# k and v in two runs of five tokens per partition pair, and k^T v from 20 matmuls of 128 rows

## The chip, the cores and the metric

One core of a Trainium2 chip runs the whole program. The metric is the device time of one execution in microseconds; the kernel before has a median of 1215.24 us over three runs (1215.23 to 1216.68).

## What is computed

Linear attention without a softmax feeds two feed-forward blocks. The change touches the attention alone: for each of 4 x 8 heads, 576 tokens of width 64.

```python
def _attn_ref(q, k, v, g_norm):          # (4, 8, 576, 64) each
    kv = np.einsum('bhsd,bhse->bhde', k, v)
    out = np.einsum('bhsd,bhde->bhse', q, kv)
    rms = np.sqrt(np.mean(out * out, axis=-1, keepdims=True) + 1e-06)
    return (out / rms * g_norm).astype(np.float32)

def reference(...):
    x = attention, as (2304, 512)
    x = _moe_ref(x)      # x @ w_in, h * clip(h + 3, 0, 6) / 6, @ w_out; 512 -> 2048 -> 512
    return _moe2_ref(x)  # 4 experts, 512 -> 1024 -> 512, weighted by domain_probs
```

## The kernel before

The attention runs in eight stages (NHB = 2 B), each of four heads of one batch. Loads, products and the rest are issued in an order written out by hand (`manual_schedule`) on PE, ACT, DVE and SP; GpSimd is left out of that order.

`att_load(i)` brings q, k and v of stage i, each with one load of 576 KB. Head pair r lies in the free dimension; the head's parity x and a group of nine tokens (CJ = 9) make the partition: partitions 0 to 63 hold the even head, 64 to 127 the odd one, and each has nine consecutive tokens of 64 values (2304 bytes). Six buffers are used in turn, so stage i + 2 reuses those of stage i. `paced` makes a load wait, from the twelfth on, for an earlier load to have landed, so that some three are under way; the weights of the first feed-forward block (`load_raw`) are in the same order of loads.

`att_q(i)` transposes q on PE. `att_kv(i)` forms k^T v: for each of nine tokens j, two parities x and two pairs r one matmul of 64 rows by 64 columns, 36 in all, accumulated in PSUM (`kvp`); the half of the partitions that a result lands on is half[x ^ r], so that the four quarters of the array are used in turn. In float32 each matmul is two passes in the trace, 72 in all. ACT copies the result to `kvd`, `att_out(i)` multiplies q by it, `att_rms(i)` normalises on ACT and DVE, and `att_x(i - 1)` transposes the stage before into the feed-forward block's operands (xH, xL).

Stage i of the loop does, in this order on PE: att_out(i), att_q(i + 1), att_kv(i + 1), then a part of a feed-forward tile (`ff_mm`, `ff_in`) or filler matmuls (`warm`), and att_x(i - 1). On SP stand att_load(i + 2) and some weight loads. `convert(n)` turns raw weights into operands, on ACT and DVE, with two of its steps on GpSimd for the first three halves (POOLED, lines 171 and 174). After the eighth stage the rest of the feed-forward blocks follows.

Of the kernel before, what the change touches and what calls it, by code (L numbers as in the profile page):

```python
# [8 lines left out]
F32 = mybir.dt.float32  # L9
# [3 lines left out]
ALU = mybir.AluOpType  # L13
AX = mybir.AxisListType
# [3 lines left out]
def kernel(  # L18
# [18 lines left out]
    nc = tc.nc  # L37
    B, H, S, D = q.shape
    NT, DM = out.shape
    E = moe2_w1.shape[0]  # L40
    P = 128
# [5 lines left out]
    CP = P // 2  # L47
    CJ = S // CP
    CB = TB // CP
    HH = H // 2  # L50
    NP = HH // 2
# [10 lines left out]
    LAG = 3  # L62
    RATE = (4200, 3000, 2600, 2900, 0)
    FMAX = 3.0e38
    PADL, PADR = 232, 248

    const = ctx.enter_context(tc.tile_pool(name="const", bufs=1))
    sp = ctx.enter_context(tc.tile_pool(name="sp", bufs=1))
# [28 lines left out]
    ident = const.tile([P, P], F32, name="ident")  # L97
    three = const.tile([P, 1], F32, name="three")
    eps4 = const.tile([P, 1], F32, name="eps4")
    gcol = const.tile([P, 1], F32, name="gcol")  # L100
    dp = const.tile([P, B, CJ, E], F32, name="dp")
    psum_e = const.tile([P, B, CJ], F32, name="psum_e")
    prob = const.tile([P, NTT, E], F32, name="prob")
# [12 lines left out]
    FREE, NEAR = 11, 13  # L116
    flow = []

    def paced(dma):
        flow.append(dma.ins)  # L120
        if len(flow) > FREE and not done[0]:
            tc.add_manual_dep(
                dma.ins, flow[-3 if len(flow) <= NEAR else -4].name,
                mybir.DependencyInfo(mybir.DependencyClass.Sync, mybir.DependencyReason.DATA), reason="paced")

    todo = [(n, h) for n in range(len(ftiles)) for h in range(2)]

    def load_raw():
        if not todo:
            return  # L130
        n, h = todo.pop(0)
        u, f = ftiles[n]
        g = sum(UNITS1[:u]) + f
        r = rawp.tile([P, KD * P, 2], U32, tag="raw", name="raw")
        if h == 0:
            paced(nc.sync.dma_start(
                out=r.rearrange("p (c f) w -> p c (f w)", c=KD),
                in_=moe_w_in.bitcast(U32)[:, 2 * g * P:2 * (g + 1) * P].rearrange("(c p) f -> p c f", p=P)))
        else:
            paced(nc.sync.dma_start(  # L140
                out=r.rearrange("p e w -> p (e w)"), in_=moe_w_out.bitcast(U32)[g * P:(g + 1) * P, :]))
        raw[n, h] = r
# [40 lines left out]
    st = {}  # L183
    natile = [0]

    def att_load(i):
        b, hf = divmod(i, 2)
        t = {}
        for nm, src in (("q", q), ("k", k), ("v", v)):
            m = natile[0] % 6  # L190
            natile[0] += 1
            pool, tag = (accp, "acc") if m < 5 else (wp, f"w{m - 1}")
            t[nm] = pool.tile([P, NP, CJ, D], F32, tag=tag, name=f"{nm}in")
            paced(nc.sync.dma_start(
                out=t[nm].rearrange("p r j d -> p r (j d)"),
                in_=src[b, hf * HH:(hf + 1) * HH].rearrange("(r x) (s j) d -> (x s) r (j d)", x=2, j=CJ),
            ))
        st[i] = t


    half = [slice(x * D, (x + 1) * D) for x in range(2)]
# [33 lines left out]
    def att_kv(i):  # L235


        t = st[i]
        kvp = t["kvp"]
        for j in range(CJ):  # L240
            for x in range(2):
                for r in range(NP):
                    nc.tensor.matmul(  # L243
                        kvp[half[x ^ r], r, :D], lhsT=t["k"][half[x], r, j, :], rhs=t["v"][half[x], r, j, :],
                        start=(j == 0), stop=(j == CJ - 1))
        nc.scalar.activation(out=kvd[i % 2][:, 0], in_=kvp[:, :, :D], func=AF.Copy)
        for y in range(2):
            nc.scalar.activation(out=kvd[i % 2][half[y], 1], in_=kvp[half[1 - y], :, :D], func=AF.Copy)
# [183 lines left out]
    start = {}  # L432
    last = {}
# [5 lines left out]
    done = [False]  # L439
# [32 lines left out]
    def warm(starts):  # L472
        z = psa.tile([P, DM], F32, tag="a0", name="zp")
        for o in starts:
            nc.tensor.matmul(z, lhsT=zero[:, o:o + P], rhs=zero, start=True, stop=True)

    warm((0,) * 8)

    att_load(0)
    load_raw()  # L480
    make_identity(nc, ident)
    nc.gpsimd.memset(three, 3.0)
    nc.gpsimd.memset(eps4, 0.25e-6)

    nc.scalar.activation(out=gcol, in_=three, func=AF.Sqrt)
    att_load(1)
    load_raw()
    nc.sync.dma_start(out=gcol[0:D, :], in_=g_norm.rearrange("(p o) -> p o", o=1))
# [5 lines left out]
    with tc.manual_schedule(engines=engines):  # L494
        qc = att_q(0)
        for x in qc[:2]:
            x()
        warm((0,) * 4)
        att_kv(0)
        qc[2]()  # L500
        warm((0,) * 2)
        conv(6)
        for i in range(NHB):
            if i + 2 < NHB:
                att_load(i + 2)
# [4 lines left out]
            if i == NHB - 2:  # L510
                for y in range(2):
                    nc.sync.dma_start(
                        out=dp[half[y]],
                        in_=moe2_domain_probs.rearrange("(b s j) e -> s b j e", b=B, j=CJ))
# [9 lines left out]
            if nxt:  # L524
                att_kv(i + 1)
                qc[2]()
            fin = [nop] * 4
            kvp = st[min(i + 1, NHB - 1)]["kvp"]
# [66 lines left out]
        for y in range(2):  # L595
            h = half[y]
            for jp in range(2):
                j = slice(2 * y + jp, CJ - 1, 4)
                nc.vector.tensor_tensor(
                    out=prob[h, :B * HH].rearrange("p (b a) e -> p b a e", b=B)[:, :, 2 * jp:2 * jp + 2],  # L600
                    in0=dp[h, :, j], in1=psum_e[h, :, j].unsqueeze(3).to_broadcast([D, B, 2, E]), op=ALU.mult)
            nc.vector.tensor_tensor(
                out=prob[h, B * HH:], in0=dp[h, y::2, CJ - 1],
# [239 lines left out]
    first = build(0)  # L843
# [70 lines left out]
```

## Time and profile before

| | us |
|---|---|
| median of three runs | 1215.24 |
| the profiled execution's own time | 1216.68 |
| span of the profiled execution | 1214.9 |
| eight k^T v products (line 243), first and last start | 8.2 and 62.8 |

The span is what the profiler's records cover; the time of an execution has 1.8 us around it. The profile shows one execution. Its parts are the busy time of each engine, the same by stretches, the chain of work that ended last followed back from the end, what each engine waited for, and the transfers with their packets. PE's weight loads (PEld) run beside its matmuls (PE). "issue" stands for time in which an engine waited for nothing that the profile shows.

### The profile page before, as it was taken

The page shows a single profiled execution, that of the slowest core. Times are in us where ns is not written, and L with a number is a line of the kernel's source. Part 1 is how long each engine was busy: PE and PEld are TensorE (multiplying, and loading weights), DVE is VectorE, ACT ScalarE, POOL GpSimd, SP SyncE. Part 2 cuts the span into 40 slices and gives each one's busy share as a digit, 9 for nine tenths or more (in the row PEclk, how much of TensorE's full clock was granted, in tenths as well). Part 3 has the DMA queues.
Part 4 walks back from the last instruction along what each step waited for, and adds up shares of the span by engine and source line. Part 5 has one row for each costly group of instructions (what it writes and reads, how often), then busy time and mean ns, then how long its engine had stood idle before and what let it go on. Part 6 is the DMA issues. An engine that isn't in the chain of part 4 may idle for free.

```text
span 1214.9 us, 17426 instructions
## 1 busy us (share of the span) xinstructions
PE 1193.9 (98%) x6999; PEld 1053.5 (87%) x6999; DVE 770.4 (63%) x1455; ACT 581.9 (48%) x1116; POOL 8.9 (1%) x16
## 2 busy tenths in 40 slices
PE   7899999999999999999999999999999999999997
PEld 6778888888888899999999889999999899999996
DVE  5889999953533755565656585656565856565652
ACT  5776555622422434444444554444445644444441
POOL 2000000000000000000000000000000000000000
PEclk9999999999999999999999999999999999999999
DMA  8812222300200012222111132222222422221202
GB/s 287 290 36 70 87 87 74 100 1 1 70 1 1 1 35 71 70 70 70 70 69 62 61 105 69 70 70 70 70 70 70 122 70 70 70 70 70 70 1 52
DMA packets 59345, 87.18 MB, mean 72 GB/s; under 512 B 3712, under 2 KB 36480, under 8 KB 59264
## 3 DMA queue, kind: packets, MB, share of 16 engines
q1 hardware_dynamic: 59264, 86.07, 21.6%
q8 instruction: 55, 0.90, 0.3%
q14 instruction: 26, 0.21, 0.1%
HBM read 81.34 MB, written 4.72 MB: 71 GB/s over the span
## 4 chain that ended last, share of the span: by engine, by line
PE 93%; DVE 3%; DMA 2%; ACT 1%; issue 1%; SPq 0%; DVEq 0%
PE po L748 32%; PE po L388 15%; PE qa L781 14%; PE qb L781 14%; PE ph L353 5%; PE ph L355 5%; PE ph L354 5%; DMA vin<-in_v_dram 2%; DMA qin<-in_q_dram 1%; DVE xl L311 1%; DVE acc L764 1%; PE kvp L243 0%; DVE r L367 0%; DVE ssq L274 0%; ACT xh L310 0%
## 5 line engine op out<-in xcount | busy, mean ns | idle before, releaser
L748 PE MATMUL po<-wout,g 128*128 128x512 f32 x1728 | 402.1, 390 | 0.0
L748 PEld LDWEIGHTS po<-wout,g 128*128 128x128 f32 x1728 | 323.6, 188 | 65.4
L781 PE MATMUL qb<-xs,win 128*128 128x384 f32 x1008 | 203.4, 336 | 1.2 <-ACT us L822 1.2
L781 PE MATMUL qa<-xs,win 128*128 128x384 f32 x1008 | 203.1, 336 | 0.0
L388 PE MATMUL po<-gH,w 128*128 128x512 f32 (+1 forms) x632 | 191.3, 368 | 0.2 <-ACT gH L369 0.2
L781 PEld LDWEIGHTS qb<-xs,win 128*128 128x128 f32 x1008 | 178.1, 188 | 4.0 <-ACT us L822 1.8
L781 PEld LDWEIGHTS qa<-xs,win 128*128 128x128 f32 x1008 | 178.3, 188 | 2.2 <-ACT us L822 0.2
L655 DVE TENSOR_TENSOR wout<-raw,wout 128x512 fp32r<-128x512 f32 x96 | 62.2, 688 | 171.2 <-ACT wout L654 171.2
L654 ACT ACTIVATE wout<-raw 128x512 fp32r<-128x512 f32 x96 | 55.4, 624 | 226.7 <-PE po L748 226.7
L388 PEld LDWEIGHTS po<-gH,w 128*128 128x128 f32 x632 | 115.7, 188 | 20.5 <-ACT gH L369 0.6
L353 PE MATMUL ph<-xh,w 128*128 128x512 f32 (+1 forms) x320 | 118.4, 370 | 0.0
L354 PE MATMUL ph<-xl,w 128*128 128x512 f32 (+1 forms) x320 | 117.9, 368 | 0.0
L355 PE MATMUL ph<-xh,w 128*128 128x512 f32 (+1 forms) x320 | 117.8, 368 | 0.0
L388 PE MATMUL po<-gL,w 128*128 128x512 f32 (+1 forms) x316 | 116.3, 368 | 0.0
L366 ACT ACTIVATE r<-ph,three 128x512 f32<-128x512 f32 (+1 forms) x80 | 51.5, 643 | 135.0 <-PE ph L355 134.8
L367 DVE SCALAR_TENSOR_TENSOR r<-r,ph 128x512 f32<-128x512 f32 (+1 forms) x80 | 50.6, 632 | 89.3 <-ACT r L366 88.8
L811 DVE SCALAR_TENSOR_TENSOR g<-sums,g 128x384 fp32r<-128x384 f32 x96 | 53.6, 558 | 81.4 <-ACT g L808 81.4
L808 ACT ACTIVATE g<-cs 128x384 fp32r<-128x384 f32 x96 | 50.4, 525 | 63.5 <-DVE cs L824 54.4
L654 ACT ACTIVATE win<-sums 128x512 fp32r<-128x512 f32 x96 | 60.7, 633 | 40.2 <-DVE sums L667 37.8
L811 DVE SCALAR_TENSOR_TENSOR g<-cs,g 128x384 fp32r<-128x384 f32 x96 | 53.4, 556 | 27.3 <-ACT g L808 27.3
L353 PEld LDWEIGHTS ph<-xh,w 128*128 128x128 f32 x320 | 60.3, 188 | 10.4
L369 ACT ACTIVATE gH<-r 128x512 fp32r<-128x512 f32 (+1 forms) x80 | 47.1, 589 | 46.1 <-DVE r L367 46.1
(129 smaller groups left out, 1275.4 us busy)
## 6 DMA issues: line engine op xcount, KB each, us to landing
raw<-in_moe_w_dram SPq DMA_DIRECT2D x96, 512.0 KB, 4.1
raw<-in_moe_w_in_dram SPq DMA_DIRECT2D x16, 512.0 KB, 3.7
raw<-in_moe_w_out_dram SPq DMA_DIRECT2D x16, 512.0 KB, 3.5
qin<-in_q_dram SPq DMA_DIRECT2D x8, 576.0 KB, 5.3
kin<-in_k_dram SPq DMA_DIRECT2D x8, 576.0 KB, 6.2
vin<-in_v_dram SPq DMA_DIRECT2D x8, 576.0 KB, 6.3
out_dram<-acc SPq DMA_DIRECT2D x36, 128.0 KB, 2.3
dp<-in_moe_domain_probs_dram SPq DMA_DIRECT2D x2, 36.0 KB, 4.2
```

What stands on the lines that cost most here:

```text
L353: nc.tensor.matmul(ph, lhsT=w[:, 0, c, :], rhs=xH[t][:, c, :], start=(c == 0), stop=False)
L354: nc.tensor.matmul(ph, lhsT=w[:, 0, c, :], rhs=xL[t][:, c, :], start=False, stop=False)
L355: nc.tensor.matmul(ph, lhsT=w[:, 1, c, :], rhs=xH[t][:, c, :], start=False, stop=(c == KD - 1))
L366: lambda: nc.scalar.activation(out=r, in_=ph, func=AF.Relu, bias=three[:, 0:1]),
L367: lambda: nc.vector.scalar_tensor_tensor(out=r, in0=r, scalar=6.0, in1=ph, op0=ALU.min, op1=ALU.mult),
L388: nc.tensor.matmul(po_t[u, t][o], lhsT=lhsT, rhs=rhs, start=(f == 0 and m == 0), stop=(f == UF[u] - 1 and m == 2))
L654: nc.scalar.activation(out=dst[0], in_=src, func=AF.Copy)
L655: nc.vector.tensor_tensor(out=dst[1], in0=src, in1=dst[0].bitcast(F32), op=ALU.subtract)
L748: nc.tensor.matmul(ps[i], lhsT=lhsT, rhs=w[:, f, y], start=(j == 0 and f == 0 and m == 0), stop=(j == FP - 1 and f == 1 and m == 2))
L781: nc.tensor.matmul(bank, lhsT=w[:, wy, AOP[m], c], rhs=xs[m][:, xy, c], start=first and n == 0, stop=n == 5, skip_group_check=True)
L808: nc.scalar.activation(out=g[f][:, 0, t], in_=src, func=func)
L811: nc.vector.scalar_tensor_tensor(out=g[f][:, 1, t], in0=src, scalar=0.0, in1=g[f][:, 0, t].bitcast(F32), op0=ALU.max, op1=ALU.subtract)
```

## The change

k and v of a stage are held in [128, 4 heads, 5 tokens, 64]: two neighbouring partitions share nine tokens, the even one holds tokens 0 to 4 and the odd one 4 to 8. Each head has a load of its own, 128 rows of 1280 bytes, so k and v take four loads of 160 KB each. The fifth token of the nine is there twice; GpSimd multiplies slot 0 of k by a column `even` that is 1 on even partitions and 0 on odd ones, in place. The product is 5 slots x 2 pairs x 2 heads = 20 matmuls that use all 128 rows and 64 columns; slot 0 comes last. `paced` counts four loads as one group. The identity is made ahead of the first loads, since `even` is summed from it on DVE. q is loaded as before.

```diff
-    PADL, PADR = 232, 248
+    PADL, PADR = 224, 248
...
+    even = const.tile([P, 1], F32, name="even")
...
-    def paced(dma):
-        flow.append(dma.ins)
-        if len(flow) > FREE and not done[0]:
+    def paced(dma, first=True, last=True):
+        if first and len(flow) >= FREE and not done[0]:
             tc.add_manual_dep(
-                dma.ins, flow[-3 if len(flow) <= NEAR else -4].name,
+                dma.ins, flow[-2 if len(flow) < NEAR else -3].name,
                 mybir.DependencyInfo(mybir.DependencyClass.Sync, mybir.DependencyReason.DATA), reason="paced")
+        if last:
+            flow.append(dma.ins)
...
+    JG, JP = CJ // 2 + 1, CJ // 2
...
+            if nm != "q":
+                t[nm] = pool.tile([P, HH, JG, D], F32, tag=tag, name=f"{nm}in")
+                for h in range(HH):
+                    first = src[b, hf * HH + h, 0, 0:1]
+                    dma = nc.sync.dma_start(
+                        out=t[nm][:, h].rearrange("p j d -> p (j d)"),
+                        in_=bass.AP(first.tensor, first.offset, [[CJ * D, CP], [JP * D, 2], [1, JG * D]]))
+                    paced(dma, h == 0, h == HH - 1)
+                continue
...
-        for j in range(CJ):
-            for x in range(2):
-                for r in range(NP):
+        nc.gpsimd.tensor_scalar(
+            out=t["k"][:, :, 0, :], in0=t["k"][:, :, 0, :], scalar1=even[:, 0:1], scalar2=None, op0=ALU.mult)
+        for j in (*range(1, JG), 0):
+            for r in range(NP):
+                for x in range(2):
                     nc.tensor.matmul(
-                        kvp[half[x ^ r], r, :D], lhsT=t["k"][half[x], r, j, :], rhs=t["v"][half[x], r, j, :],
-                        start=(j == 0), stop=(j == CJ - 1))
+                        kvp[half[x ^ r], r, :D], lhsT=t["k"][:, 2 * r + x, j, :], rhs=t["v"][:, 2 * r + x, j, :],
+                        start=(j == 1), stop=(j == 0))
...
+    make_identity(nc, ident)
+    nc.vector.tensor_reduce(
+        out=even, in_=ident.rearrange("p (s y) -> p y s", y=2)[:, 0, :], axis=AX.X, op=ALU.add)
     att_load(0)
     load_raw()
-    make_identity(nc, ident)
```

## Rows read from the trace of the kernel before

**Rows 1.** The page, part 1: busy us of each engine, share, instructions.

```profile
PE 1193.9 (98%) x6999; PEld 1053.5 (87%) x6999; DVE 770.4 (63%) x1455; ACT 581.9 (48%) x1116; POOL 8.9 (1%) x16
```

**Rows 2.** Stretches: us, length, busy us (instructions) per engine, granted clock, DMA share, GB/s.

```profile
20.00:25.00 5.00, 3.12 (x87) 2.58 (x85) 4.40 (x11) 2.98 (x9) 2.55 (x2) 1.00 0.63 202
...
50.00:55.00 5.00, 5.00 (x164) 4.41 (x163) 4.84 (x9) 3.30 (x7) 1.01 (x1) 1.00 0.94 333
...
100.00:110.00 10.00, 10.00 (x45) 8.27 (x45) 9.97 (x19) 5.58 (x9) 0.00 (x0) 1.00 0.34 101
```

**Rows 3.** The chain that ended last, in order of time: start us, us, what.

```profile
22.33 7.89 DMA vin<-in_v_dram
...
30.36 1.28 PE kvp L243 x72
...
34.58 1.42 issue
...
38.45 1.01 PE kvp L243 x57
39.46 1.67 issue
41.13 0.46 PE kvp L243 x15
...
62.15 0.43 issue
```

**Rows 4.** Waits of PE in the first 70 us: in total us, times, longest.

```profile
PE kvp L243 <- DMA vin<-in_v_dram: 3.6, 3, 1.7
```

**Rows 5.** PE's instructions up to the two holes (stretches), and PE's instruction queue, 0 to 70.

```profile
28.10:34.70 6.60, 6.04 (x126) 5.05 (x127) 4.22 (x10) 4.68 (x11) 0.00 (x0) 1.00 0.79 237
35.90:39.70 3.80, 3.46 (x127) 3.11 (x127) 2.80 (x7) 2.71 (x6) 0.00 (x0) 1.00 0.89 291
...
q8 instruction: 10, 0.16, 1.1%
```

**Rows 6.** The product's line: one stage as a stretch; all passes, ns min/median/max; waits.

```profile
30.30:31.70 1.40, 1.28 (x72) 1.17 (x72) 1.00 0.88 300
...
L243 PE MATMUL kvp<-vin,kin x576: 213/218/268, 8.2 to 62.8; 64*64 64x64 f32 x192
...
L243 PEldq EVENT_SEMAPHORE  x8: 51/51/51, 7.7 to 60.2; - x8
```

**Rows 7.** Eight passes on 128 rows and columns: timeline, and their weight loads.

```profile
69.20 1.05 PE L564 MATMUL kvp<-ident 128*128 128x128 f32 x8
...
L564 PEld LDWEIGHTS kvp<-ident x8: 187/192/192, 69.0 to 69.9; 128*128 128x128 f32 x8
```

**Rows 8.** Packets, 2.5 to 7 us, and of one lone load, 92 to 97: count, MB, share.

```profile
DMA packets 792, 1.69 MB, mean 375 GB/s; under 512 B 41, under 2 KB 73, under 8 KB 792
...
q1 hardware_dynamic: 792, 1.69, 98.4%
...
q1 hardware_dynamic: 528, 0.52, 34.0%
```

**Rows 9.** SP's timeline, two issues; the second one's us from issue to landing.

```profile
1.23 0.46 SPq L194 DMA_DIRECT2D kin<-in_k_dram  x1
...
31.52 0.37 SPq L194 DMA_DIRECT2D vin<-in_v_dram  x1
...
vin<-in_v_dram SPq DMA_DIRECT2D x1, 576.0 KB, 6.7
```

**Rows 10.** GpSimd's timeline: start us, us, what.

```profile
1.35 0.10 POOL L482 MEMSET three<- 128x1 f32 x1
...
1.51 0.29 POOL masks.py:199 TENSOR_SCALAR_AFFINE_SELECT ident<-ident 128x128 f32<-128x128 f32 x1
...
53.99 1.27 POOL L171 TENSOR_TENSOR r<-r,x 128x512 f32<-128x512 f32 x1 [30.61 <-ACT qT L228]
```

**Rows 11.** Waits of SP's queue in the first 90 us: in total us, times, longest.

```profile
SPq L194 <- DMA kin<-in_k_dram: 18.5, 5, 9.4
...
SPq L489 <- DMA kin<-in_k_dram: 0.4, 1, 0.4
```

## The prediction

> **What bounds the kernel now.** I read the page's first part first: PE is busy 98% of the span, DVE 63%, ACT 48% [rows 1]. Whatever an edit saves on PE's path is therefore worth its full length, and so is whatever it adds. Then the busy time by stretches: from 100 us on PE has no idle time (10.00 of 10), while in the attention stretch it has gaps (3.12 of 5 between 20 and 25 us, with the DMA engines at 0.63) [rows 2]. The edit lies wholly in that stretch, the first 63 us, so the question is by how much the eighth k^T v product ends earlier or later; all behind it is unchanged and moves with it.
>
> The chain of work in order of time tells what limits that stretch [rows 3]. Up to 30.2 us it is loads: the fourth v, issued at 22.33, took 7.89 us to land, and the product of that stage began at 30.36. PE waited for v three times, 3.6 us in all [rows 4]. After that the chain is compute: PE, ACT, DVE in turn, and between 50 and 55 us DVE is busy 4.84 of 5 [rows 2]. In between stand three holes named "issue", where PE waited for nothing that the profile shows: 1.42, 1.67 and 0.43 us [rows 3]. The middle one cuts a product in two, after 57 of its 72 passes. PE has 126 matmuls and 127 weight loads in the stretch that ends with the first hole and 127 and 127 in the one that ends with the second; the instruction queue brought 10 packets in the first 70 us, 0.16 MB, 16 KB each [rows 5]. So I read the holes as PE running out of instructions: each packet carries some 254, and bursts of tiny matmuls use them up faster than the busy DMA engines bring them.
>
> **Part by part.** Stages are numbered from 0; "product i" is att_kv(i), "v(i)" its load.
>
> The matmuls. Each is two passes in the trace: 72 become 40 per stage, with as many weight loads; 64 instructions fewer per stage, 512 in all, two instruction packets. Time is another matter. A product now takes 1.28 us [rows 6]; less the 0.22 us of the last pass, 72 passes in rounds of four quarters are 18 rounds of 0.059 us. The new passes use all 128 rows and half the columns, so at best two run side by side: 20 rounds, 20 x 0.059 + 0.22 = 1.40 us, 0.12 us **longer**. If the halves take turns, 40 x 0.059 + 0.22 = 2.58 us. Below 1.28 I see no reason to go: the time of a round is that of one pass. I take 1.40, by the row of the eight 128-row passes: they took 1.05 us together, (1.05 - 0.28) / 7 = 0.11 us apart, though one weight load lasts 0.19 [rows 7]; so weight loads lie under other passes even when every row is in use.
>
> The Trainium skill ("TensorE: Matmul & The Clock Gate", Part 3, The mechanism) speaks against that: a weight load overlaps a running matmul only when the row group differs, and here it never does. By that rule the product goes to the upper end and the result to the rival "halves take turns"; the 0.11 us above is against it, but for full-width passes only.
>
> The loads. k and v go from one load of 576 KB each to four of 160 KB, 640 KB together, in packets of 1280 bytes instead of 2304. Between 2.5 and 7 us the engines spent 98.4% of 16 x 4.5 us on 792 packets, of which 73 were shorter: 93 to 99 ns for a 2304-byte one, say 96. A lone 1 KB-packet load spent 34.0% of 16 x 5 us on 528: 51.5 ns [rows 8]. On the line between, 1280 bytes cost 60 ns, so a load is 512 x 60 / 16 = 1.93 us of every engine against 256 x 96 / 16 = 1.54: +0.40. By bytes alone it is 64/576 of 1.54: +0.17. The 1 KB row is of a lone load and need not hold in a full queue, so I take the middle, 0.28. Before v(3) lands lie eight such loads: 30.22 + 2.2 = 32.4 us (31.6 to 33.4). Before v(4), ten: it was issued at 31.52 and took 6.7 [rows 9], so 38.2 + 2.8 = 41.0 (39.9 to 42.2).
>
> SP's queue. Six more issues per stage, 0.37 to 0.48 us each [rows 9]: nine are 3.3 to 4.3 us of a stage of some 7. They stay ahead of the engines, which need 1.8 us for the four loads that SP issues in 1.5 to 1.9. The two g_norm loads, the raw weights and the next q stand behind them; none is wanted before the second stage, so nothing is charged. The paced waits ask for the same groups as before.
>
> GpSimd. The zeroing is 128x256 elements. The rows bound it: 0.29 us (128x128 select) and 1.27 (128x512 with two inputs) [rows 10]; I take 0.6, half the latter. It starts when k has landed, v lands later, and the token it touches is multiplied last, so it is covered; uncovered it costs up to 0.6 a stage. DVE's mask sum runs in the first microseconds, where DVE has nothing else to do. Extra waits on PE: a product has one event wait of 0.051 us now [rows 6]; eight loads and GpSimd could make it eight, between 0 and 0.36 us; I take 0, since earlier passes are in flight meanwhile.
>
> The sum. Product 3 starts at 32.4 + 0.14 = 32.5 and ends at 33.9 (31.64 now). From there to product 4 it is 38.45 - 31.64 = 6.8 us now, 5.4 without the hole of 1.42: 39.3. With fewer instructions per stage I expect that hole and the later two to go. But v(4) lands at 41.0, so **the load takes back what the holes gave**: product 4 runs from 41.1 to 42.5, against 41.59 now (39.46 + 1.67 + 0.46): +0.9. Behind it DVE is the limit until product 7; two more products on the path add 2 x 0.12, the hole of 0.43 goes: +0.9 + 0.24 - 0.43 = **+0.7 us**. The profiled execution took 1216.68 us (span 1214.9 and 1.8 around it) and would take 1217.4; it lies 1.4 over the median, so by the median of 1215.24 I predict 1215.9. With the ends of the load price, and the event waits at 0.36 on two products at the upper one, this case runs from 1214.8 (v(4) at 39.9) to 1217.8 (42.2).
>
> A second rule of the skill bears on the holes ("Runtime: NRT & Kernel Launch", Instruction fetch mechanics): blocks of 16 KiB, 256 instructions, are fetched ahead, and crossing into the next is mostly hidden. The packet size agrees with the rows; "mostly hidden" does not if my reading of the three holes is right. If they were something else and stayed, product 4 would end near 44.2 and the time be about 1218.
>
> **The rivals.** A measurement of this kernel tells some 0.2%, 2.4 us, from no change.
>
> Halves take turns (slower). Place: every product; price 1.3 us instead of 0.12 each; it decides once the passes on the two column halves don't overlap. On the path it counts for products 4, 5 and 7; for 3 it is hidden under the wait for v(4). 3 x 1.2 on top of the forecast: 1219.5. For it speaks that no row shows two half-width passes together; against it rows 7.
>
> Eight loads in flight (slower). The second g_norm load, tenth issue, needs nothing of k and yet waited 0.4 us for a k load, the second issue [rows 11]; so a load waits until the one eight issues before it has landed. With nine issues a stage this becomes the bound as soon as eight small loads, 1.3 MB, are less than the way from issue to landing holds; today the paced groups keep about 1.8 MB under way and SP waits 18.5 us for k alone [rows 11]. At 1.3 MB every 6 us instead of 333 GB/s [rows 2] the loads of q(3) to v(4) would lose up to 6 us; half of that is 1218.9.
>
> Zeroing queued behind conversion (slower). GpSimd's weight conversion runs from 53.99, 1.27 us and as much again [rows 10]; product 6 runs at 53.6. If k(6) is zeroed after it, the product ends some 2.1 us later: 1218.0. Against it: GpSimd ran the memset of three before the select of make_identity, which stands ahead of it in the program [rows 10], so its order follows readiness.
>
> Loads keep pace (faster). All three holes go, 3.5 us, and v(3) and v(4) land no later than today's chain wants them, because there are fewer instruction packets on the same engines and the 37% idle share between 20 and 25 us [rows 2] takes up the extra bytes: -3.5 + 0.4, 1212.1.
>
> That the kernel doesn't do what it says would show in the counts alone (320 passes, 64 loads of 160 KB) and I give it nothing.
>
> **How the numbers follow.** Forecast 0.57 (all counted within 0.2%), halves in turn 0.10, eight loads 0.13, zeroing late 0.06, loads keep pace 0.14. Faster 0.14, same 0.57, slower 0.29. The range 1212.8 to 1219.2 leaves out the halves' case and the outer part of the fast one.
>
> **What would show it.** Right: products of 1.40 us; v(3) landing near 32.4 and v(4) near 41.0; no "issue" hole over 0.5 us in the chain between 30 and 63 us; the first pass of product 4 released by v, not by the transposes. Wrong: products over 2 us; SP waiting for loads of the same stage; k's zeroing after 54 us named as releaser of product 6; holes still there; or v(4) in by 39 us.

## The result: 7.6 us slower, and the profile after

The changed kernel takes 1222.84 us (median of 4 runs, 1221.72 to 1225.19) against 1215.24: a ratio of 1.0063, 95% interval 1.0045 to 1.008. The prediction was 1215.9, within 1212.8 to 1219.2; the change is slower by some ten times the +0.7 us of the sum. The profiled execution is the slowest of the four, 1225.19 us with a span of 1223.4.

The page, part 1, of the kernel after (against [rows 1]):

```profile
PE 1203.3 (98%) x6743; PEld 1059.8 (87%) x6743; DVE 771.0 (63%) x1456; ACT 581.4 (48%) x1116; POOL 16.9 (1%) x24
```

PE has 256 matmuls and as many weight loads fewer, as counted, and is yet busy 9.4 us longer. The stretches say why; columns as in [rows 2].

```profile
15.00:20.00 5.00, 3.93 (x47) 3.23 (x45) 4.37 (x11) 1.40 (x5) 3.43 (x3) 0.69 0.83 247
20.00:25.00 5.00, 5.00 (x83) 3.90 (x84) 2.58 (x5) 3.47 (x9) 0.27 (x1) 0.63 0.98 337
50.00:55.00 5.00, 4.87 (x70) 3.85 (x72) 3.83 (x10) 3.22 (x10) 0.80 (x1) 1.00 0.85 271
70.00:75.00 5.00, 4.27 (x80) 3.61 (x81) 4.70 (x11) 4.52 (x12) 0.00 (x0) 0.65 0.02 7
100.00:110.00 10.00, 10.00 (x50) 8.33 (x49) 9.78 (x27) 7.57 (x16) 0.00 (x0) 1.00 0.18 55
```

From 100 us on PE has no idle time in either kernel. In the attention the granted clock falls to 0.63 and 0.65, where before it stood at 1.00; there PE is busy for longer with the same work. Between 50 and 55 us the transfers are at 271 GB/s where they were at 333, and DVE, which was the limit there, has 1.2 us to spare.

The chain that ended last shows the cause in its first 32 us (start us, us, what):

```profile
1.22 0.68 SPq L201
1.95 0.60 SPq L201
...
5.83 0.60 SPq L201
6.48 0.59 SPq L138
7.12 7.14 DMA qin<-in_q_dram
14.28 0.53 SPq L201
...
17.25 5.55 DMA qin<-in_q_dram
22.82 4.19 DMA vin<-in_v_dram
27.09 0.54 SPq L201
...
31.58 3.50 DMA vin<-in_v_dram
```

Line 201 is the load of one head. Before, the chain at this place is three loads up to 30.2 us, then PE; the third stands in [rows 3], and the first two are

```profile
2.85 7.77 DMA qin<-in_q_dram
10.63 11.22 DMA vin<-in_v_dram
```

Now it is SP putting out load after load, 0.60 us each, up to 7.1 us. Then it is a landing: q(1) goes out at 7.12 and lands at 14.26, and 0.02 us later SP issues the last head of v(1), which is the eighth load after it. At 17.25 q(2) goes out, 5.55 us later the eighth load after that. So two things hold SP: the time of an issue, and a load's wait for the load eight issues before it. The second acted before the change too: v(2), the eighth load after q(1), went out at 10.63 us, when q(1) had landed (10.62).

SP's issues of the loads of k and v, 0 to 66 us (count, duration ns min/median/max, first and last start us):

```profile
L201 SPq DMA_DIRECT2D kin<-in_k_dram x32: 541/601/1387, 1.2 to 58.0; - x32
L201 SPq DMA_DIRECT2D vin<-in_v_dram x32: 534/605/1254, 3.9 to 60.9; - x32
```

All of them take 0.53 us or more, where the large loads took 0.46 and 0.37 [rows 9]. Before, the last load of stage 1 was issued at 4.0 us; now it is at 14.3. What that means for the data shows in the transfers of the first 15 us, before and after (one row each):

```profile
DMA packets 2497, 4.76 MB, mean 317 GB/s; under 512 B 253, under 2 KB 765, under 8 KB 2496
```

```profile
DMA packets 2855, 3.76 MB, mean 251 GB/s; under 512 B 238, under 2 KB 2342, under 8 KB 2854
```

One MB less has arrived, although the changed kernel wants more. The products end later by 1.37, 3.89, 4.96, 4.82, 3.19, 3.97, 4.82 and 3.51 us than before, from product 0 to 7: the delay is there by product 2 and later stages hold it. PE waits for v eight times now [rows 4]:

```profile
PE kvp L258 <- DMA vin<-in_v_dram: 4.8, 8, 1.0
```

How the clock falls, by two microseconds (columns as in [rows 2]):

```profile
14.00:16.00 2.00, 1.31 (x10) 1.04 (x10) 1.93 (x4) 1.60 (x4) 0.00 (x0) 1.00 0.99 351
16.00:18.00 2.00, 1.31 (x10) 1.00 (x12) 1.67 (x6) 0.79 (x2) 1.89 (x2) 0.72 0.90 305
18.00:20.00 2.00, 2.00 (x35) 1.88 (x33) 1.73 (x4) 0.01 (x1) 1.54 (x2) 0.50 0.73 156
```

PE had run with gaps for q(1) and v(1) (1.31 of 2 us), and then works at 0.50, the lower of the two levels (1.2 GHz). Up to 58.4 us the chain is loads and issues, with one zeroing between them (1.08 us at 41.04), so this dip lies beside them and is a consequence, not the cause; that it costs nothing there was not tried by itself.

At the end of the attention a second thing stands, on GpSimd:

```profile
62.78 0.93 POOL kin L253
63.71 1.24 POOL r L173
64.98 1.65 POOLq L926
66.66 0.03 ACT w L178
```

The zeroing of k(7) stands ahead of two steps of the weight conversion. ACT waits 2.7 us for the second, and att_out(7) and what follows it wait with ACT. From the end of product 7 to the first matmul behind the attention (line 581) it is 12.0 us in this execution (66.55 to 78.56); before it was 6.2 (63.04 to 69.20). PE idled here (busy 3.79 of the 5 us up to 70), and then the clock fell again, to 0.65 and 0.67 up to 80 us. This dip does stand in the chain: eight transposes of att_x take 1.90 us, where eight took 0.87 before (first line before, second after):

```profile
33.22 0.87 PE px L318 x8
```

```profile
74.52 1.90 PE px L333 x8
```

So in this execution, the slowest of the four, 5.8 of the 9.4 us by which that matmul starts later arise behind product 7. How much of that holds in the median, e1_order tells.

### The profile page after: what moved, and what is told of

It is laid out like the page before. It is cut to its first block, busy times and chain, and to the rows that moved or that the text cites. A ratio compares the mean times of both kernels' runs of the same rounds, so it can differ in the third digit from the quotient of the medians.

```text
span 1223.4 us, 17029 instructions
## 1 busy us (share of the span) xinstructions
PE 1203.3 (98%) x6743; PEld 1059.8 (87%) x6743; DVE 771.0 (63%) x1456; ACT 581.4 (48%) x1116; POOL 16.9 (1%) x24
## 4 chain that ended last, share of the span: by engine, by line
PE 91%; DMA 3%; DVE 2%; SPq 2%; ACT 1%; issue 1%; POOL 0%; POOLq 0%; DVEq 0%; ACTq 0%
PE po L765 32%; PE po L403 15%; PE qa L798 14%; PE qb L798 14%; PE ph L368 5%; PE ph L369 5%; PE ph L370 5%; SPq L201 1%; DMA vin<-in_v_dram 1%; DMA qin<-in_q_dram 1%; DVE acc L781 1%; DMA kin<-in_k_dram 0%; DVE r L382 0%; ACT xh L325 0%; POOL kin L253 0%
## 5 line engine op out<-in xcount | busy, mean ns | idle before, releaser
L368 PEld LDWEIGHTS ph<-xh,w 128*128 128x128 f32 x320 | 60.6, 189 | 10.5
L370 PEld LDWEIGHTS ph<-xh,w 128*128 128x128 f32 x320 | 60.6, 189 | 10.1
```

The lines of the kernel that those rows point to most:

```text
L368: nc.tensor.matmul(ph, lhsT=w[:, 0, c, :], rhs=xH[t][:, c, :], start=(c == 0), stop=False)
L370: nc.tensor.matmul(ph, lhsT=w[:, 1, c, :], rhs=xH[t][:, c, :], start=False, stop=(c == KD - 1))
```

## The experiments

Theories: **S**, the loads' number and SP's queue; **G**, GpSimd's order; **B**, the extra bytes and shorter packets. Each ratio is to runs of the kernel before on the same chip, with its 95% interval.

| run | loads of k and v a stage | median issue of these, us | us | ratio | MB in 15 us |
|---|---|---|---|---|---|
| after | 8 of 160 KB | 0.60 | 1222.84 | 1.0063 (1.0045 to 1.008) | 3.76 |
| e1_order | 8 of 160 KB | 0.60 | 1220.79 | 1.0048 (1.0031 to 1.0065) | 3.87 |
| e2_nozero | 8 of 160 KB | 0.60 | 1221.16 | 1.0047 (1.0029 to 1.0065) | 3.86 |
| e3_two | 4 of 320 KB | 0.61 | 1215.44 | 1.0003 (0.9993 to 1.0012) | 4.81 |
| e4_split | 8 of 144 KB, 64 partitions | 0.59 | 1224.07 | 1.0062 (1.0039 to 1.0084) | 3.78 |
| e5_matmul | 2 of 576 KB | 0.37 | 1214.31 | 0.9984 (0.9975 to 0.9992) | 4.83 |
| e6_pool | 2 of 576 KB | 0.37 | 1214.81 | 0.9995 (0.9986 to 1.0004) | 4.71 |
| e7_halves | 4 of 320 and 256 KB, 64 partitions | 0.61 | 1222.96 | 1.0064 (1.0052 to 1.0076) | 3.41 |
| e9_tiny | 2 of 576 KB, 6 of 64 B | 0.42 (64 B) | 1223.71 | 1.0068 (1.0055 to 1.0081) | 3.57 |
| e10_96 | 2 of 576 KB, 96 partitions | 0.32 | 1220.5 | 1.0048 (1.0034 to 1.0061) | 3.90 |
| e11_first | 4 of 320 KB | 0.61 | 1214.54 | 0.9999 (0.999 to 1.0008) | 4.79 |
| e12_late | 4 in stages 0, 1; then 8 | 0.60 | 1218.69 | 1.0035 (1.0022 to 1.0048) | 4.56 |
| e13_early | 8 in stages 0, 1; then 4 | 0.61 | 1218.98 | 1.0032 (1.0022 to 1.0042) | 4.01 |
| e14_act | as e13, v's early ones on ACT | 0.61 | 1217.22 | 1.0022 (1.0012 to 1.0033) | 4.33 |
| e15_four | 8 of 160 and 128 KB | 0.43 | 1216.91 | 1.0014 (1.0005 to 1.0023) | 4.10 |
| e16_pairs | 4 of 288 KB | 0.43 | 1214.35 | 0.9991 (0.9982 to 1.0) | 4.71 |
| e17_over | 8 of 160 KB | 0.43 | 1217.48 | 1.0019 (1.001 to 1.0028) | 4.15 |
| e18_strides | 8 of 160 KB, 2 engines | 3.2 | 1390.23 | 1.143 (1.1415 to 1.1446) | 1.12 |
| e19_inner | 8 of 160 KB | 0.60 | 1220.38 | 1.004 (1.0027 to 1.0054) | 3.98 |

### GpSimd: order mended (e1_order), no zeroing (e2_nozero), zeroing alone (e6_pool)

```diff
+        if i == NHB - 1:
+            tc.add_manual_dep(z.ins, pooled[1, 0].name, DependencyInfo(NoSync, DATA), reason="order")
```

> The changed kernel (1222.84 us) with one edge more in the order of GpSimd: the zeroing of the eighth k stands behind the last conversion step, where the trace of after had it ahead. Theory G (GpSimd's queue): conversion then no longer waits for k(7) to land, ScalarE's wait of 2.71 us for GpSimd goes, PE doesn't run dry behind product 7 and its granted clock stays at 1.00 between 70 and 80 us (0.65 to 0.67 in after): 3.5 to 5 us less, about 1218 to 1219.5. Theory S (SP's issues are all of the loss): the order on GpSimd is off the path, the time stays within 1 us of 1222.8.

```diff
-        nc.gpsimd.tensor_scalar(
-            out=t["k"][:, :, 0, :], in0=t["k"][:, :, 0, :], scalar1=even[:, 0:1], scalar2=None, op0=ALU.mult)
```

> The changed kernel with the zeroing left out (the fifth of each nine tokens counts twice in k^T v; all else is done). Theory G: the same gain as with the order mended, and besides it the holes before the last passes of a product go, 0.3 to 0.7 us each where they lie on the path: 1217 to 1219. Theory S: product 7 still ends about 66 us and the time stays above 1221.

In the kernel before:

```diff
+        nc.gpsimd.tensor_scalar(
+            out=t["k"][:, :, :2, :], in0=t["k"][:, :, :2, :], scalar1=one[:, 0:1], scalar2=None, op0=ALU.mult)
-        for j in range(CJ):
+        for j in (*range(2, CJ), 0, 1):
```

> The kernel before, with GpSimd multiplying the first two tokens of k (128x256 elements, as the zeroing) by a column of ones, in place, and these tokens last in the product. GpSimd's part alone. Theory G, GpSimd's queue costs on the path by itself: about 2 us, as ordering it behind the conversion gave back: 1216.7 to 1218.0. Theory S, the loads make the whole loss and GpSimd's wait lies under that of the load where the loads come in time: 1215.2 to 1216.0.

In e1_order product 7 ends at 65.93 and the first matmul behind the attention starts at 72.16: 6.2 us, as before, and the granted clock is 1.00 from 70 to 80 us. The median is 2 us better, between the ranges of G and S, and e2_nozero's is no more than that, in the range of S. Three quarters of the loss stand with nothing on GpSimd: G is at most the smaller part, some 2 us that the intervals don't part from none. e6_pool shows nothing (0.9995): where the loads come in time, 0.93 us of GpSimd a stage lies under the load of v.

### Two loads in place of four (e3_two)

```diff
-                for h in range(HH):
-                    first = src[b, hf * HH + h, 0, 0:1]
+                for y in range(2):
+                    first = src[b, hf * HH, y * JP, 0:1]
                     dma = nc.sync.dma_start(
-                        out=t[nm][:, h].rearrange("p j d -> p (j d)"),
-                        in_=bass.AP(..., [[CJ * D, CP], [JP * D, 2], [1, JG * D]]))
+                        out=t[nm][y::2].rearrange("p h j d -> p h (j d)"),
+                        in_=bass.AP(..., [[CJ * D, CP], [S * D, HH], [1, JG * D]]))
```

> The changed kernel with two loads for each k and v instead of four, one of the even and one of the odd partitions (320 KB each, the same bytes in the same 1280-byte packets). Theory S: five issues a stage instead of nine, SP leaves the chain, product 7 ends at 63 to 64 us instead of 66.6; with GpSimd's part left as it is, 1218 to 1220. Theory B (bytes and packet size, as in the prediction): no change, 1222 to 1224, product 7 still near 66.5.

Measured 1215.44: the whole loss is gone with the same layout, bytes, packet length and zeroing. B falls. It is better than S had allowed, although GpSimd now stands on the path (what PE waited for: us in total, times, longest):

```profile
PE kvp L258 <- POOL kin L253: 4.1, 2, 2.5
```

The zeroing of k(1) and k(2) runs behind the weight conversion there and cuts products 1 and 2 in two.

### Four loads in the kernel before, to 64 partitions (e4_split) and to 128 (e15_four); two (e16_pairs)

```diff
+                for h in range(HH):
+                    r, x = divmod(h, 2)
+                    dma = nc.sync.dma_start(
+                        out=t[nm][x * CP:(x + 1) * CP, r].rearrange("p j d -> p (j d)"),
+                        in_=src[b, hf * HH + h].rearrange("(s j) d -> s (j d)", j=CJ))
```

> The kernel before with one part of the change alone: k and v are loaded head by head, four loads of 144 KB each, in the old layout and the old 2304-byte packets, with no byte more. Theory S: nine issues a stage at about 0.65 us each bind SP, product 7 ends 2 to 4 us later than 63.0 and the time is 1217 to 1219. Theory B: same bytes, same packets, 1215 to 1216.

Measured 1224.07, more than S had allowed. I took it for the whole proof, wrongly: its loads go to 64 partitions, and e7_halves (below) shows such loads to be slow by themselves; in e4_split packets of 2304 bytes took 131 ns (median) up to 15 us, against 93 in the kernel before. So once more with 128 partitions, r a head pair, js tokens 0 to 4 or 5 to 8, and with two loads, a head pair each:

```diff
+                        out=t[nm][:, r, js].rearrange("p j d -> p (j d)"),
+                        in_=src[b, hf * HH + 2 * r:hf * HH + 2 * r + 2].rearrange(
+                            "x (s j) d -> (x s) j d", j=CJ)[:, js].rearrange("p j d -> p (j d)"))
```

> The kernel before with four loads for each of k and v that all go to 128 partitions: head pair 0 or 1, tokens 0 to 4 or 5 to 8 of nine (160 and 128 KB, rows of 1280 and 1024 bytes); layout, bytes and product as before. e4_split brought each head to 64 partitions, and e7_halves showed such loads to be slow by themselves, so it can't stand for the number of loads alone. Theory S, the number of loads: 1219 to 1224. Rival, the slowness of e4_split was that of its 64 partitions, and the changed kernel's has other sources: 1215 to 1217.5.

> The kernel before with two loads for each of k and v, a head pair each (288 KB, 128 partitions, rows of 2304 bytes as before). Theory S, with five issues a stage SP keeps its lead: 1214.5 to 1216.5, as the two-load kernels; if each issue more than three costs by itself, a third of the loss: 1217 to 1218.5.

Two loads cost nothing (0.9991), four cost 0.14%: below what S expected, a quarter of the loss of the change. The issues of k's loads in e15_four, to be held against those of the kernel after:

```profile
L199 SPq DMA_DIRECT2D kin<-in_k_dram x32: 328/430/987, 1.2 to 54.2; - x32
```

0.43 us in place of 0.60: with 0.05 between them nine take some 4.3 us and not 5.9 of a stage of some 7.

### Bytes or issue time (e17_over, e18_strides, e19_inner)

e17_over takes the overlap of the changed kernel into e15_four (js = tokens 0 to 4 or 4 to 8); the others change its address pattern alone:

```diff
-                        in_=src[b, ...].rearrange("x (s j) d -> (x s) j d", j=CJ)[:, js]...   # e17: one stride
+                        in_=bass.AP(..., [[2 * S * D, 2], [CJ * D, CP], [1, 5 * D]]))          # e18: 2 outside
+                        in_=bass.AP(..., [[CJ * D, CP], [2 * S * D, 2], [1, 5 * D]]))          # e19: 2 inside
```

> e15_four with the overlap of the changed kernel: four loads for each of k and v to 128 partitions, all of 160 KB in rows of 1280 bytes, the fifth of nine tokens brought twice; the product reads it once, 72 passes as before, nothing on GpSimd. So number, size, bytes and packets are those of the changed kernel's loads; what differs is the address pattern: these rows have one stride, and such a load took SP 0.43 us in e15_four, where a head's load in the changed kernel, whose source has two strides, took 0.60. Theory SI, SP's time to issue is what makes four loads dear: as e15_four, 1215.5 to 1218. Theory B4, the bytes count once eight small loads are all that is under way: 1219.5 to 1223.

> e17_over with one thing else: the rows of a load have two strides in place of one, as in the changed kernel, because a load takes heads 0 and 2 or 1 and 3 of the four instead of neighbours (k^T v then goes to another head's q; the work is the same). Number, size, bytes, packets, partitions and the 72 passes are those of e17_over. If a second stride is what makes the issue take 0.60 us: theory SI, SP's issue time is the loss, 1220 to 1224; theory B4 or any cause that isn't the issue, as e17_over, 1216 to 1218.5. If the issue stays at 0.43 us: 1216 to 1218.5 in any case, and the two aren't parted.

> e17_over with the address pattern of the changed kernel's loads: 64 steps of nine tokens outside, two steps inside, here between heads 0 and 2 or 1 and 3, so that the rows of two heads lie on alternating partitions (the product mixes them; the work is the same). In e18_strides the two steps were outermost, its loads ran on two of the 16 engines at 49 GB/s, and it told nothing of the issue. Number, size, bytes, packets, partitions and the 72 passes are those of e17_over. Expected of the issue: 0.60 us in place of 0.43, as in the changed kernel. Theory SI, that time makes the loss: 1220 to 1224. Theory B4 or another cause: as e17_over, 1216 to 1218.5.

e17_over: 1.0019 against 1.0014, so the bytes and the length of the packets cost nothing that shows (0.05%, with 0.13 either way). e18_strides told nothing of the question: between 20 and 60 us its transfers mostly ran at some 50 GB/s with an eighth of the engines busy, and an issue took 3.2 us:

```profile
L201 SPq DMA_DIRECT2D kin<-in_k_dram x32: 516/3172/4556, 1.2 to 207.1; - x32
```

The Trainium skill ("DMA: Bandwidth & Descriptors", Rules for kernel authors) says that the slowest dimension sets the number of engines, and one of less than 16 confines a transfer to at most as many; the trace agrees (outermost 2: 2 of 16 engines by their share). e19_inner has the steps the other way round and its issues, here those of k, are those of the changed kernel:

```profile
L201 SPq DMA_DIRECT2D kin<-in_k_dram x32: 541/602/1685, 1.2 to 59.8; - x32
```

It takes 1.004 (1.0027 to 1.0054) against 1.0019 (1.001 to 1.0028). Same loads, same bytes, same partitions, same product: 0.17 us more on SP for each issue is 2.6 us (0.21%) of the time, though the two intervals overlap by 0.0001. Packets of 1280 bytes take 55 ns (median) in both, so the pattern makes the issue longer and not the transfer.

That it is the second stride, as I had thought, the other runs don't bear out. The loads of the kernel before have two strides in their source as well (128 steps, two rows in each), and those of e4_split have one (64 steps of one row); in this order:

```profile
L194 SPq DMA_DIRECT2D kin<-in_k_dram x8: 367/368/478, 1.2 to 48.4; - x8
```

```profile
L198 SPq DMA_DIRECT2D kin<-in_k_dram x32: 465/592/702, 1.2 to 57.0; - x32
```

In all runs loads of k and v whose source has 64 outer steps take 0.59 to 0.61 us to issue, with one row a step (e4_split), two (after, e19_inner) or four (e3_two, e7_halves), and those with 128 take 0.37 to 0.43. No run changed this number alone, so the cause of the longer issue stays open.

The chain of e19_inner begins as that of the kernel after does:

```profile
1.97 0.60 SPq L201
...
7.13 6.71 DMA qin<-in_q_dram
13.86 0.54 SPq L201
...
16.97 6.63 DMA qin<-in_q_dram
```

SI is borne out, at the lower end of its range, and with 1.004 e19_inner stands where e2_nozero stands (1.0047), which has the same issues and no zeroing.

### Issues without bytes (e9_tiny)

```diff
+            if nm != "q":
+                for h in range(HH - 1):
+                    nc.sync.dma_start(out=tiny[:, 2 * i + (nm == "v"), h, :], in_=src[b, hf * HH, :16, :1])
```

> The kernel before with three more loads of 64 bytes (16 partitions of 4 bytes, never used) ahead of each load of k and v: nine issues a stage on SP as in the changed kernel, and no bytes to speak of. It parts the two ways in which the number of loads can cost. Theory SI, SP's time to issue (0.60 us each, back to back, 5.9 us a stage): 1219 to 1224, as with the loads of a head each. Theory SF, eight loads under way hold too few bytes when they are small (each load waits until the one eight issues before has landed): here the large loads are as large as before and any eight issues hold two or three of them, the tiny ones land soon, so 1215.2 to 1217.0.

Measured 1223.71, in SI's range, but by the other way. Its tiny loads take SP 0.42 us, so SP would keep up; the chain says

```profile
0.73 4.04 DMA qin<-in_q_dram
4.79 5.81 DMA vin<-in_v_dram
...
26.22 2.30 PE kvp L247 x69
```

v(0) is the eighth load behind q(0) and goes out when q(0) has landed (4.77), where before it was issued at 1.73; v(1) goes out at 13.43 (4.02 before). The large loads stand behind tiny ones that wait for large ones. Part of the 8 us is the clock: it stood at 0.50 from 25 to 30 us, and there 69 passes of product 2 take 2.30 us, where 72 of product 3 took 1.28 before [rows 3].

### Half the early loads on another queue (e12_late, e13_early, e14_act)

```diff
+                for y in range(2) if i < 2 else ():      # e12_late; e13_early has i >= 2: two loads, as e3_two
+                    ...
-                for h in range(HH):
+                for h in () if i < 2 else range(HH):
...
-                    dma = nc.sync.dma_start(             # e14_act, from e13_early
+                    dma = (nc.scalar if nm == "v" else nc.sync).dma_start(
```

> The changed kernel with two loads (even and odd partitions, 320 KB each) for each of k and v in stages 0 and 1, and a load for each head from stage 2 on. Both theories take the number of loads as the cause. Theory E, the loss is made at the start: in the changed kernel the last load of v(1) goes out at 14.3 us, before at 4.0, and product 2 is already 5 us late; later stages add little: 1215.2 to 1217.5. Theory C, it is made in every stage, nine issues of 0.60 us each and only eight under way: 1220 to 1223.

> The other half: a load for each head in stages 0 and 1, two loads for each of k and v from stage 2 on. Theory E: products 0 to 2 as late as in the changed kernel (4 to 5 us), little won back: 1219 to 1222.5. Theory C: the stages from 2 on run faster than the loads were wanted and win the delay back, 1215.2 to 1218.

> The kernel of e13_early (a load for each head in stages 0 and 1, two loads from stage 2 on; 4 us slower than before) with the eight loads of v in stages 0 and 1 issued from ScalarE's queue in place of SP's. The number of loads is the same, SP has eight issues fewer in the first 14 us. It parts two ways in which the number of loads can cost. Theory SI, SP's time to issue (0.60 us each): v(1) goes out some 4 us earlier, products 0 and 1 end within 1.5 us of before: 1215.0 to 1217.0. Theory SF, the wait of each load for the landing of the one eight issues before: the loads still come in groups of eight, v(1) goes out no earlier than about 10 us, products 1 and 2 stay 2 us or more late: 1217.5 to 1220.

The first two lie between E and C: 0.35% with the small loads in stages 2 to 7 alone, 0.32% in stages 0 and 1 alone, together 0.67 against 0.63. Half of the loss is made at the start. e14_act is at 0.22%, between SI's range and SF's; its interval overlaps that of e13_early. Its chain:

```profile
2.58 5.32 DMA kin<-in_k_dram
7.91 6.35 DMA qin<-in_q_dram
```

The two queues have eight loads out by 3.5 us; the third head of k(0), issued at 2.58, must land (7.90) before q(1), eighth behind it, goes out at 7.91. Product 1 ends 2.5 us late (18.54). So when issuing is made quicker the wait for the eighth load before binds.

### The matmuls alone (e5_matmul), and with two loads (e11_first)

```diff
-        for j in range(CJ):
+        for j in range(5):
...
-                        ..., lhsT=t["k"][half[x], r, j, :], rhs=t["v"][half[x], r, j, :],
+                        ..., lhsT=t["k"][:, r, j + 4 * x, :], rhs=t["v"][:, r, j + 4 * x, :],
```

> The kernel before with its loads and its layout, but the product made of 20 matmuls of 128 rows (five slots instead of nine tokens); its operands are then not those of the reference, the attention's product is another one. It has the matmul part of the change alone. As the prediction counted it: products of 1.40 us in place of 1.28, the three holes (1.42, 1.67, 0.43 us) gone, v(4) landing where it did, near 38.2 us: of the first two holes some 2 us come through to product 4, the third on top, less 0.24 for the longer products: 1212.5 to 1214.0. Rival, the holes were not instructions running out, or what they give is lost to the next load: 1215.0 to 1215.7. Rival, the halves of the columns take turns: products of 2.58 us and over 1217.5.

```diff
+        if i in (1, 2):   # e3_two, with the conversion on GpSimd behind the zeroing
+            tc.add_manual_dep(pooled[0, i - 1], z.ins.name, DependencyInfo(NoSync, DATA), reason="order")
```

> Two loads for each of k and v in all stages, and GpSimd's order mended where it held products 1 and 2 in two by 1.66 and 2.46 us: the zeroing of k(1) and k(2) stands ahead of the weight conversion. Theory S (loads few enough, so the product's own gain comes through): products 1 and 2 undivided, three holes gone, the matmul part alone gave about 2 us: 1212.5 to 1214.5. Rival, the loads of 320 KB (1.28 MB against 1.15 for k and v of a stage, in shorter packets) take the gain: product 3 still waits for v(3) near 33.7 us: 1214.8 to 1216.

e5_matmul is at 0.9984, about 1.9 us faster; its 1214.31 us lie just above the range of the matmul part (1212.5 to 1214.0). Products 3, 5 and 7 are one piece each (chain):

```profile
28.60 1.39 PE kvp L243 x40
...
42.56 1.32 PE kvp L243 x40
...
56.63 1.31 PE kvp L243 x40
```

No hole longer than 0.14 us stands between 28 and 60 us of its chain. e6_pool, with 72 passes, has one of 1.46 us. The three holes of the kernel before and this one end 1.2 to 1.5 us after a packet of 16 KB has landed in the instruction queue of [rows 5] (at 34.55, 39.94 and 61.10 us, and at 37.23 in e6_pool), which fits the reading that PE had run out of instructions. e11_first is at 0.9999, as the rival said; nothing cuts its products, and nothing is won, since PE waits for v:

```profile
PE kvp L263 <- DMA vin<-in_v_dram: 6.3, 5, 1.9
```

### Loads to a part of the partitions (e7_halves, e10_96)

```diff
+                        out=t[nm][half[y], :, :JG - y]...   # e7: tokens 0 to 4 of nine to partitions 0 to 63, 5 to 8 to 64 to 127
...
+                    out=t[nm][:S // JG]...                  # e10: JG = 6, 96 partitions, one load
+                    in_=src[b, hf * HH:(hf + 1) * HH].rearrange("h (s j) d -> s h (j d)", j=JG)))
```

> The changed kernel with another layout: partitions 0 to 63 hold tokens 0 to 4 of nine, partitions 64 to 127 tokens 5 to 8, two loads for each of k and v (320 and 256 KB, 576 in all as before), no token twice and nothing on GpSimd; the fifth slot's matmuls use 64 rows. Theory S (the number of loads is the loss): five loads a stage take SP some 3 us of 7, no loss: 1213.5 to 1215.5, the lower end if what the vanished holes give comes through. Theory B (bytes or packets of 1280 bytes): as little, since the bytes are those of before, but the packets are half as long: 1215.5 to 1217.5. If the layout of 128 rows itself cost something it would be above 1217.

> Another way to one load per tensor: k and v of a stage on 96 partitions with six tokens each (1536-byte rows, 576 KB, no token twice, nothing on GpSimd), the product from 24 matmuls of 96 rows, 48 passes, about 24 x 0.059 + 0.22 = 1.64 us. Theory S (the number of issues is the loss): three a stage as before: 1213 to 1215.5. Rival P, from the kernel with halves, where loads to 64 of the 128 partitions moved some 240 GB/s with all engines busy against some 400: a load to 96 partitions moves some 300 GB/s, under the 333 of the stretch from 50 to 55 us: 1217 to 1222.

Measured 1222.96 and 1220.5. With e7_halves S should have seen no loss and B little: both missed. The layout of 128 rows is not the cause, for e3_two has it too. Columns as in [rows 2], the last two DMA share and GB/s; e7_halves from 15 to 20 us, then e3_two from 10 to 15:

```profile
15.00:20.00 5.00, 1.44 (x20) 1.20 (x21) 4.53 (x12) 2.35 (x6) 2.53 (x2) 1.00 1.08 259
```

```profile
10.00:15.00 5.00, 3.71 (x90) 2.80 (x85) 2.82 (x6) 3.88 (x9) 0.69 (x1) 1.00 1.07 400
```

The engines are as busy, the rows of like length (1280 and 1024 bytes against 1280), and the rate is 259 GB/s against 400. The difference is where a load goes: to 64 neighbouring partitions, or to every second one of 128. Packets of 1280 bytes took 95 ns (median) up to 15 us in e7_halves and 85 from 20 to 60, against 55 in e3_two. e10_96 from 40 to 55 us:

```profile
DMA packets 2314, 3.88 MB, mean 258 GB/s; under 512 B 108, under 2 KB 1732, under 8 KB 2310
...
q1 hardware_dynamic: 2310, 3.83, 105.4%
```

This is rival P, and slower than the three quarters of 400 that I had assumed, although q's loads to 128 partitions are among these.

## Why the prediction was wrong

**The step that failed** is "SP's queue": "They stay ahead of the engines, which need 1.8 us for the four loads that SP issues in 1.5 to 1.9." A head's load takes SP 0.60 us, not 0.37 to 0.48: four take 2.6 us with the gaps between them, and SP is behind the engines. I took the duration from rows of the large loads [rows 9], whose source has 128 outer steps; the new pattern has 64 and takes 0.17 us more an issue (e17_over against e19_inner). SP's 77 issues up to the last of v take 47.9 of the first 61.4 us of the kernel after; before, 29 took 12.8 of 50.2. Then "nothing is charged" asked whether SP keeps pace in a running stage, and not what its lead is for: before, the loads of k and v of stages 0 and 1 were all issued by 4.5 us, now by 14.8. The runs put the term at +2.3 us for eight loads at 0.43 us (e17_over, 0.19%) and +2.6 more for the 0.60 (e19_inner, 0.40%). The signs fail with it: v(3) landed at 35.1 us, not near 32.4, and the last head of v(4), due near 41.0, was not issued before 40.37.

**The rival "eight loads in flight"** had a mechanism that acts, with a chance of 0.13 and at the wrong place. I put it at the loads of q(3) to v(4); it holds SP from the load that goes out at 7.1 us on, and a queue of nine issues a stage with eight under way has no more than one stage in flight (e9_tiny, e14_act). Issue time and this wait alternate in the chain, and how the 4.9 us divide between them stays open.

**"The load takes back what the holes gave"** held, as a balance. The holes go with the 72 passes (e5_matmul), and are worth 1.9 us where the loads are those of before; with two longer loads each 0.1 (e11_first), so these take 1.8 back. Where SP's queue binds, as in the changed kernel, no gain shows: e2_nozero, with 40 passes, is at 1.0047 and e19_inner, with 72, at 1.004. Had k and v been brought by two loads each, the forecast of "the same" would have stood (e3_two).

**GpSimd**: the zeroing takes 0.92 us, not 0.6, within the bounds, and is covered where the loads come in time (e6_pool). The rival "zeroing queued behind conversion" came in two forms. In e3_two it cut products 1 and 2, as described. In the changed kernel it is the reverse: the zeroing of k(7) stands first and the conversion, with ACT behind it, is late; the medians give some 2 us (0.63 less 0.47%), unresolved. That GpSimd's order follows readiness was no argument: the loads set what is ready, and these moved. 4.9 for the loads and 2 for this make 6.9 of the 7.6 us; by the intervals the first is known to some 1.6 us either way and the second to 2.9.

**The matmuls** were right: 1.39 us (1.40 forecast), so halves lie side by side. The Trainium skill's rule ("TensorE: Matmul & The Clock Gate", Part 3, The mechanism), that a weight load overlaps a running matmul only in another row group, is not borne out: 40 passes of 0.222 us took 1.39 us, not 2.58. Nor is what the Trainium skill says of the step into the next block of instructions ("Runtime: NRT & Kernel Launch", Instruction fetch mechanics), that it is mostly hidden, if the holes are that step: with them went 1.9 us.

**Charged to nothing, and not tried alone**: the event waits on PE became four a product, 0.051 us each, and DVE's mask sum took 0.22 us at 1.81, before any load had landed. The extra bytes, +0.28 us a load in the sum, don't show by themselves (e17_over against e15_four). The price was right for the engines (a packet of 1280 bytes took 55 ns and one of 2304 bytes 93, so 512 x 55 / 16 - 256 x 93 / 16 = +0.27); that each such load delays PE by as much was wrong, as e3_two has the same packets and no loss.

## What to carry to other kernels

Before one load is cut into several, count the issues and not only the bytes: what an issue with the new address pattern costs its queue, how many loads may be under way, and when the last load of the first stages now goes out, for there the whole lead is made. Where a layout needs loads with a slow issue, two of them over all partitions did here what four could not; a load to a part of the partitions is no way out. What a shorter program gives shows only if the loads behind it don't come later.

## What the runs showed of the hardware

- SP's issue took 0.43 us for 160 KB whose source has 128 outer steps of one row, and 0.60 for the same 160 KB in 64 steps of two rows (e17_over, e19_inner); 0.59 in 64 steps of one row (e4_split), 0.61 in 64 of four (e3_two), 0.37 in 128 of two (before); 0.42 us for 64 bytes (e9_tiny). The Trainium skill ("DMA: Bandwidth & Descriptors", Issuing engines are not separate DMA queues) calls this time usually small relative to the transfer; here eight issues, 4.8 us, took longer than their 1.31 MB at 400 GB/s (3.3 us).
- With all engines busy, loads to 64 neighbouring partitions (e7_halves) or to 96 (e10_96) moved some 260 GB/s, loads to all 128 moved 375 (before, 2.5 to 7 us [rows 8]) and loads to every second of 128 moved 400 (e3_two).
- A load waited for the landing of the load eight issues before it (issued at 7.12, landed at 14.26, the eighth after it issued at 14.28 us).
- A load whose outermost dimension was 2 ran at 50 GB/s, and held SP 3.2 us at each issue.
- After gaps in its work (busy 1.31 of 2 us, twice) PE's granted clock was 0.50 from 18 to 20 us of the kernel after, with PE busy throughout.
